# First mixture of a three-stage kernel: overflow blocks of all experts in one loop behind the last expert, rows written by indirect DMA

## Chip, core and metric

The kernel runs on one core of one Trainium2 chip. The metric is the device time of one execution in microseconds, the median of several runs. Engines are named as the profile names them: PE is TensorE (PEld its weight loads, PEq its sequencer), DVE is VectorE, ACT is ScalarE, POOL is GpSimd, SP is SyncE; SP issues most of the DMAs.

## What is computed

Attention, then a mixture of experts in which each token goes to one expert, then a second mixture in which each token goes to all eight. Cut to the part that the change touches:

```python
# attention: B=4, H=8, S=576, D=64, chunks of 64   -> x of (2304, 512)

def _moe_ref(x, w_gate, w1, w2, capacity):           # first mixture, capacity = 576
    logits = x @ w_gate
    expert_idx = np.argmax(logits, axis=1)           # one of E = 8 experts
    gate_w = ...                                     # its softmax probability
    for i in range(N):                               # tokens in order
        e = expert_idx[i]
        if counts[e] < capacity:                     # a full expert drops the token
            disp[e, counts[e]] = x[i]; pos[i] = counts[e]; counts[e] += 1; keep[i] = True
    h = np.maximum(np.einsum('ecd,edf->ecf', disp, w1), 0.0)    # D=512, F=1024
    y = np.einsum('ecf,efd->ecd', h, w2)
    out[i] = gate_w[i] * y[expert_idx[i], pos[i]]    # 0 for a dropped token

def _moe2_ref(x, w_gate, w1, w2):                    # second mixture
    P = exp(x @ w_gate - max), scaled 8 times to rows and columns of equal sums
    for e in range(E):
        out += P[:, e:e + 1] * (np.maximum(x @ w1[e], 0.0) @ w2[e])
```

With the inputs that are timed, the eight experts of the first mixture get 512, 128, 466, 384, 174, 128, 320 and 192 tokens. No expert has more than 512, and no token is dropped.

## The kernel before

The kernel is a single program. Attention runs until about 134 us of the span, the first mixture until 381 us, the second until the end. All products are made in 16-bit floats with a high and a low half of each operand (names `hi`, `lo`, `hh`, `hl`), so that one exact product is three matmuls.

**First mixture.** A loop in Python (`for x in range(E)`, unrolled in the program) runs over the experts. An expert's tokens are gathered from DRAM by index (`gather`, on POOL), turned by PE (`turn`, L338), and worked on in blocks of 128 rows by `blocks`. `blocks` makes the first product with `first_product` (L353 on PE; ACT and DVE make `hh` at L358 and `hl` at L359) and the second product (L896 on PE); then ACT squares the result (L900), DVE finds a power of two as scale (L89 to L92), ACT and DVE write the two halves of the row tile (L906, L907), and SP sends the row to `x2_d` (L909) and the row's scale and token number, `rkt`, to `rk_d` (L914). In the trace, the tile `x_d` is `x2_d`. The first product goes by four groups of the 1024 hidden columns.

Each expert has, in this order: a pair of blocks that always runs (tokens 0 to 255); `further(2)` inside an If with label `m` (more than 256 tokens, L1060; expert 0 has no such If); inside it `further(3)` in an If with label `n` (more than 384, L1063); and inside that `rest()` in an If with label `o` (more than 512, L1065). `rest` is a loop over the blocks from 512 on; for expert 0 it also recomputes the first two blocks if an earlier guess about which tokens are its own had found too few; for expert 7 it also starts two loads named `heads`. Tests are made on the engines' own registers, on every engine. An engine that skips a body runs a short list of semaphore updates in the body's place, and waits there for its own work before the If to be finished; the profile puts these under the If's line (L1060, L1063, L1065). With this run's counts, L1065's test is reached by experts 0 and 2 and skips in both; L1063 skips for experts 3 and 6, L1060 for experts 1, 4, 5 and 7.

**Work woven in.** `sites` is a list of lists of Python functions: between two groups of a block's first product, and behind each second product, `blocks` calls the functions of one list. They load, scale and split the next expert's weights: `w_scale` is a matmul against a matrix of ones that sums over partitions (`over_partitions`, L177), `w_scale2` is a chain of small DVE operations on it (L205, L89 to L92, L213), `w_split` writes a weight's two halves (ACT L254 or L246, DVE L255 or POOL). The order in which these calls are written is the order on each engine; every engine works through its queue in order.

**Second mixture.** It begins with transposes on PE of the first rows (L1171, on the tiles loaded by `heads`), casts of them on ACT and DVE into tiles `x` (L1181), and first products (L1283). Its tiles lie in pools that share memory with those of the first mixture.

## Time and profile before

| | |
|---|---|
| three runs | 1741.68, 1744.98, 1749.51 us |
| median | 1744.98 us |
| the profiled execution | 1743.53 us |
| its span | 1741.8 us |
| PE busy in the span | 97% |
| DVE, ACT, POOL busy | 69%, 55%, 42% |
| granted TensorE clock, mean | 0.997 |

The span is the profiled part of one execution; 1.7 us of that execution lie outside it. "Busy" counts matmuls, vector operations and the like, not branches, semaphore operations or DMA issues. Where an engine was idle before an operation, a timeline row gives the length in brackets, and behind the arrow what ended it; an engine's name with a q (PEq, DVEq) is that engine's sequencer, and the line behind it the line of the semaphore operation or branch. [...]

### The profile page before, as it was taken

How to read it: one execution, taken by the hardware profiler on the slowest of the kernel's cores; microseconds unless marked ns; L12 is line 12 of the kernel's file. 1: busy time of each engine (PE TensorE's matmuls, PEld its weight loads, DVE VectorE, ACT ScalarE, POOL GpSimd, SP SyncE). 2: the span in 40 equal slices, each digit the busy share in tenths (PEclk: the TensorE clock that was granted, in tenths of full speed). 3: DMA queues.
4: the chain of work that ended last, by engine and by line, in shares of the span. 5: the costliest groups of instructions: out<-in, count | busy, mean ns of one | idle time of the engine just before them, and what ended most of it. 6: DMA issues, size and time to landing. Idle time of an engine off the chain costs nothing.

```text
span 1741.8 us, 33426 instructions
## 1 busy us (share of the span) xinstructions
PE 1691.9 (97%) x13203; PEld 1224.7 (70%) x13203; DVE 1199.1 (69%) x2336; ACT 953.5 (55%) x1805; POOL 726.7 (42%) x765
## 2 busy tenths in 40 slices
PE   8889999989999999999999999999999999999997
PEld 6775666655555577777777777777777767777776
DVE  7886857755578666776676767677766686677554
ACT  6976756754445554665455545455644665354431
POOL 2335644622023243553445434453534543453443
PEclk9999999999999999999999999999999999999999
DMA  9948878745242413242233224323323241323201
GB/s 227 248 142 243 228 182 195 198 113 143 82 155 94 144 53 134 65 176 85 92 129 131 87 98 148 107 86 113 130 89 133 65 174 47 131 66 126 91 34 49
DMA packets 140344, 219.17 MB, mean 126 GB/s; under 512 B 62304, under 2 KB 80832, under 8 KB 140160
## 3 DMA queue, kind: packets, MB, share of 16 engines
q1 hardware_dynamic: 134768, 199.46, 36.6%
q0 software_dynamic: 5392, 17.26, 3.6%
q8 instruction: 115, 1.88, 0.5%
q14 instruction: 69, 0.57, 0.2%
HBM read 167.56 MB, written 41.91 MB: 120 GB/s over the span
## 4 chain that ended last, share of the span: by engine, by line
PE 69%; DVE 5%; ACT 2%; issue 1%; POOL 1%; POOLq 0%; ACTq 0%; DVEq 0%
PE p_m L1283 36%; PE p_m L1379 28%; PE p_m L1427 5%; DVE wall L297 3%; DVE acc L1350 1%; ACT wall L296 1%; PE p_m L1171 0%; ACT eh L1288 0%; POOL out_dram L1361 0%; DVE el L1291 0%; ACT tq L1323 0%; DVE tq L1298 0%; POOL el L1295 0%; DVE tq L1301 0%; DVE wall L255 0%
## 5 line engine op out<-in xcount | busy, mean ns | idle before, releaser
L1283 PE MATMUL p_m<-x,wall 128*128 128x384 f16 x4032 | 667.7, 326 | 4.9 <-ACT tq L1323 4.1
L1295 POOL TENSOR_TENSOR el<-tq,eh 128x384 f16<-128x384 f32 x336 | 346.8, 1060 | 568.6 <-ACT eh L1288 567.9
L1379 PE MATMUL p_m<-wall,eh 128*128 128x256 f16 x3528 | 580.3, 273 | 0.0
L1283 PEld LDWEIGHTS <-wall 128*128 128x128 f16 x4032 | 394.3, 98 | 262.6 <-issue 8.3
L1379 PE MATMUL p_m<-wall,el 128*128 128x256 f16 x1764 | 480.8, 273 | 0.0
L1288 ACT ACTIVATE eh<-tq 128x384 f16<-128x384 f32 x540 | 274.1, 522 | 190.2 <-DVE tq L1301 101.4
L1379 PEld LDWEIGHTS <-eh 128*128 128x128 f16 x3528 | 344.3, 98 | 44.4
L1350 DVE SCALAR_TENSOR_TENSOR acc<-p_m,cf,acc 128x256 f32<-128x256 f32 (+1 forms) x378 | 175.6, 521 | 130.7 <-PE p_m L1379 130.7
L1298 DVE TENSOR_TENSOR tq<-p_m,tq 128x384 f32<-128x384 f32 x288 | 158.4, 556 | 127.9 <-PE p_m L1283 126.8
L1379 PEld LDWEIGHTS <-el 128*128 128x128 f16 x1764 | 172.6, 98 | 19.9
L1291 DVE SCALAR_TENSOR_TENSOR el<-tq,eh 128x384 f16<-128x384 f32 x204 | 175.2, 860 | 10.0 <-ACT eh L1288 8.6
L1301 DVE SCALAR_TENSOR_TENSOR tq<-tq 128x384 f32<-128x384 f32 x252 | 133.1, 553 | 2.8
L353 PEld LDWEIGHTS <-wall 128*128 128x128 f16 x1344 | 107.3, 98 | 19.3 <-issue 7.2
L1323 ACT COPY tq<-p_m 128x384 f32<-128x384 f32 x96 | 45.6, 475 | 112.4 <-PE p_m L1283 109.9
L1427 PE MATMUL p_m<-wall,eh 128*128 128x512 f16 x288 | 85.6, 379 | 0.0
L275 POOL TENSOR_TENSOR tq<-stb 128x256 f32<-128x256 f32 x56 | 48.9, 873 | 81.9 <-DVE wsumsq L184 59.0
L1336 ACT ACTIVATE tq<-tq 128x384 f32<-128x384 f32 x84 | 43.9, 522 | 69.9 <-DVE tq L1298 69.9
L353 PE MATMUL p_p<-xT,wall 128*128 128x256 f16 x672 | 75.6, 272 | 3.7 <-DMA rk_d<-rkt 1.5
L296 ACT ACTIVATE wall<-stb,wsb 128x256 f16<-128x256 f32 (+1 forms) x56 | 31.3, 606 | 87.0 <-DMA wb_d<-wall 61.5
L275 POOL TENSOR_TENSOR tq<-sta 128x256 f32<-128x256 f32 x56 | 45.0, 804 | 72.8 <-DVE wall L297 43.3
L247 POOL TENSOR_SCALAR stb<-stb,wsb 128x1024 f32<-128x1024 f32 x16 | 53.6, 3350 | 52.0 <-DVE tq L1298 45.1
L297 DVE SCALAR_TENSOR_TENSOR wall<-stb,wsb,wall 128x256 f16<-128x256 f32 (+1 forms) x56 | 38.1, 690 | 50.9 <-ACT wall L296 48.1
(283 smaller groups left out, 2115.5 us busy)
## 6 DMA issues: line engine op xcount, KB each, us to landing
x<-xt_d SPq DMA_DIRECT2D x147, 384.0 KB
wb_d<-wall SPq DMA_DIRECT2D x20, 896.0 KB
wall<-wb_d SPq DMA_DIRECT2D x20, 896.0 KB
sta<-in_moe_w_dram SPq DMA_DIRECT2D x32, 512.0 KB
stb<-in_moe_w_dram SPq DMA_DIRECT2D x32, 512.0 KB
sta<-in_moe_w_dram SPq DMA_DIRECT2D x16, 1024.0 KB
stb<-in_moe_w_dram SPq DMA_DIRECT2D x16, 1024.0 KB
xt_d<-x SPq DMA_DIRECT2D x21, 384.0 KB
```

The costliest lines, as they stand in the source:

```text
L275: nc.gpsimd.tensor_tensor(out=at(o), in0=at(u), in1=at(v), op=op)
L297: nc.vector.scalar_tensor_tensor(out=o[:, cs, 1], in0=src, scalar=m.s, in1=o[:, cs, 0], op0=ALU.mult, op1=ALU.subtract)
L353: nc.tensor.matmul(p[:, f4, :], lhsT=w[:, kk, f * 128:(f + 1) * 128], rhs=xT[:, lo + kk, 0:W], start=(n == 0), stop=(n == 3 * KD - 1))
L1283: nc.tensor.matmul(p, lhsT=wt[:, w, lw, kk, :], rhs=xt[:, lx, kk, :], start=first and n == 0, stop=n == 5, skip_group_check=not first)
L1288: nc.scalar.activation(out=hs[op][0][:, q, :], in_=src, func=AF.Relu if op in (A11, A12, A22) or plain else AF.Copy)
L1291: nc.vector.scalar_tensor_tensor(out=hs[op][1][:, q, :], in0=src, scalar=0.0, in1=hs[op][0][:, q, :], op0=ALU.max, op1=ALU.subtract)
L1295: nc.gpsimd.tensor_tensor(out=hs[op][1][:, q, :], in0=src, in1=hs[op][0][:, q, :], op=ALU.subtract)
L1298: nc.vector.tensor_tensor(out=o, in0=a, in1=b, op=ALU.add)
L1301: nc.vector.scalar_tensor_tensor(out=o, in0=a, scalar=0.0, in1=b, op0=ALU.max, op1=op)
L1350: nc.vector.scalar_tensor_tensor(out=acc[:, j, cols], in0=y, scalar=coefs[x][:, j:j + 1], in1=acc[:, j, cols], op0=ALU.mult, op1=ALU.add)
L1379: nc.tensor.matmul(bk.t[:, cols], lhsT=hs[op][lh][:, q, t * 128:(t + 1) * 128], rhs=b.q[q][:, w, lw, :], start=m in (1, 5) and q == 0 and ...
L1427: nc.tensor.matmul(y.t, lhsT=h[:, kk % 4, c * 128:(c + 1) * 128], rhs=w[:, kk, :], start=(n == 0), stop=(n == 3 * KF - 1))
```

## The change

All eight Ifs with label `o` and their `rest()` are taken out, and the branch hints that belonged to them. One If with label `r` (more than 512 tokens in any expert, or expert 0 needs its recomputation) stands behind the last expert instead. Its body is a loop over the experts; for one with work left it loads both weight matrices again, scales and splits them, and loops over its blocks from `t0` on; each block's rows are written by indirect DMA from POOL at row numbers worked out on the chip. The weights go into new tiles of the pools `stage2` and `stage_b`. `heads(gpsimd)` stands at the end of this body, and the `heads` on SP at expert 7 tests the same number.

The loop needs a small table `left` (for each expert: tokens left, first block, count, first row, count again) and the number `e_any`. They are made for every run, by two functions put into the sites of expert 4: `redo_sum` into the first list and `tables` into the third. The two operations that made `e_count` and `e_more` before are gone. `blocks` gets an argument `put`, which takes the place of the two row DMAs in the loop alone.

```diff
         def counted():
-            nc.vector.tensor_copy(e_count, p_tab[:, 256:258])
             nc.vector.tensor_scalar(out=e_redo, in0=p_tab[:, 256:257], scalar1=255.0, scalar2=float(N),
...
-        nc.vector.tensor_tensor(out=e_more, in0=e_redo, in1=p_tab[:, 256:257], op=ALU.max)
...
+        redo = const.tile([128, 3], F32, name="redo")
+
+        def redo_sum():
+            nc.vector.tensor_tensor(out=redo[:, 0:1], in0=e_redo, in1=ident[:, 0:1], op=ALU.mult)
+            hold["redo"] = over_partitions(redo[:, 0:1], 300, 1)
+
+        def tables():
+            nc.vector.tensor_copy(redo[:, 0:1], hold.pop("redo"))
+            nc.vector.tensor_reduce(out=redo[:, 1:2], in_=reg_i[:, 0:E], axis=AX.X, op=ALU.max)
+            nc.vector.tensor_tensor(out=e_any, in0=redo[:, 0:1], in1=redo[:, 1:2], op=ALU.max)
+            nc.vector.tensor_copy(left[:, :, 0], reg_i[:, 0:E])
...
             def next_count():
                 if y < E:
                     counted_next.append(count(y))
+                if y == E - 1:
+                    more.append(count(0, e_any))
...
             if x == E - 1:
-                with tc.If(rc <= N - SB):
+                with tc.If(more[0] <= 512):
                     heads(nc.sync)
...
+            if x == 4:
+                sites[0].append(redo_sum)
+                sites[2].append(tables)
...
-                rc = count(0, e_more)
+                rc = count(0)
...
+                if y == E:
+                    sites[4].append(lambda: tc.mark_branch_hint_location("r", more[0] > 512, engines=[mybir.EngineType.PE]))
...
                 with tc.If(rc > 384, label=f"n{x}"):
-                    further(3, [[lambda: skip("o")], [], []])
-                    with tc.If(rc > 512, label=f"o{x}"):
-                        rest()
+                    further(3)
...
+        more = more[0]
+
+        with tc.If(more > 512, label="r"):
...
+            with tc.For_i(0, E, 1) as e:
+                cur = cp.tile([128, 5], I32, tag="cur", name="cur", bufs=1)
+                nc.vector.tensor_copy(cur, of[:, bass.ds(e * 5, 5)])
+                with tc.If(nc.values_load(cur[0:1, 0:1], min_val=0, max_val=N) > 512):
...
+                        m.st = pool.tile([128, m.kk, m.n], F32, tag="st" + nm, name=f"st{nm}r")
+                        m.mx = smw("wmx" + nm, [128, 4])
+                        nc.sync.dma_start(out=m.st, in_=w[bass.ds(e, 1), :, :].rearrange("o (k p) n -> p (o k) n", p=128))
...
+                        for d, src in ((x2_d, row), (rk_d, to)):
+                            nc.gpsimd.indirect_dma_start(out=d[:, :], out_offset=bass.IndirectOffsetOnAxis(ap=at_i, axis=0),
+                                                         in_=src, in_offset=None)
+
+                    with tc.For_i(t0, (c + 127) // 128, 1) as t:
...
+                        blocks("r", turn(gather([idx], "xgl", 1), "xTl", "c"), 1, None, y_bank="c", put=put)
+            heads(nc.gpsimd)
```

In the program the change shows at three places. The first is PE at the start of expert 4's block pair, between the first and the second group of the first product; `wmxa` and `wmxb` are the maxima of the next expert's weights, `ones` the matrix of ones. Before:

```order
L353 LDWEIGHTS wall
L353 MATMUL p_p<-xT,wall 128x256
L177 MATMUL p_sum<-wmxa,ones_85 128x4 [waits Activation_49]
L177 MATMUL p_sum<-wmxb,ones_85 128x4 [waits DVE_49]
L353 LDWEIGHTS wall
L353 MATMUL p_p<-xT,wall 128x256 [waits PE_49]
```

After:

```order
L353 LDWEIGHTS wall
L353 MATMUL p_p<-xT,wall 128x256
L177 MATMUL p_sum<-wmxa,ones_85 128x4 [waits Activation_49]
L177 MATMUL p_sum<-wmxb,ones_85 128x4 [waits DVE_49]
L177 MATMUL p_sum<-redo,ones_85 128x1 [waits DVE_49]
L353 LDWEIGHTS wall
L353 MATMUL p_p<-xT,wall 128x256 [waits PE_49]
```

A third small matmul stands in PE's queue, ahead of the second group, and it waits for DVE.

The second is DVE in the same stretch, where it works on the next expert's weights (`wall<-sta` is a piece of the low half of its first matrix) and makes `hl` of each group. Before:

```order
L213 TENSOR_TENSOR iw<-wia,wib 128x1 [waits DVE_49]
L255 SCALAR_TENSOR_TENSOR wall<-sta_4321,wsa,wall 128x1024 [waits Activation_49]
L359 SCALAR_TENSOR_TENSOR hl<-p_p,hh 128x512 [waits Activation_49]
L255 SCALAR_TENSOR_TENSOR wall<-sta_4321,wsa,wall 128x1024 [waits Activation_49] x2
L359 SCALAR_TENSOR_TENSOR hl<-p_p,hh 128x512 [waits Activation_49]
L255 SCALAR_TENSOR_TENSOR wall<-sta_4321,wsa,wall 128x1024 [waits Activation_49]
```

After:

```order
L213 TENSOR_TENSOR iw<-wia,wib 128x1 [waits DVE_49]
L255 SCALAR_TENSOR_TENSOR wall<-sta_3574,wsa,wall 128x1024 [waits DMAHW6_49,Activation_49]
L948 TENSOR_TENSOR redo<-e_redo,ident 128x1
L359 SCALAR_TENSOR_TENSOR hl<-p_p,hh 128x512 [waits Activation_49]
L255 SCALAR_TENSOR_TENSOR wall<-sta_3574,wsa,wall 128x1024 [waits DMAHW7_49,Activation_49]
L255 SCALAR_TENSOR_TENSOR wall<-sta_3574,wsa,wall 128x1024 [waits DMAHW2_49,Activation_49]
L359 SCALAR_TENSOR_TENSOR hl<-p_p,hh 128x512 [waits Activation_49]
L255 SCALAR_TENSOR_TENSOR wall<-sta_3574,wsa,wall 128x1024 [waits DMAHW3_49,Activation_49]
L952 COPY redo<-p_sum 128x1 [waits DVE_49]
L953 TENSOR_REDUCE redo<-reg_i 128x1
L954 TENSOR_TENSOR e_any<-redo 128x1 [waits DVE_49]
L955 COPY left<-reg_i 128x8
```

The operation that the new matmul waits for (L948) stands behind the first L255 and ahead of the second group's `hl`; the eleven operations of `tables` (L952 to L962, the first four of them shown) stand between the fourth L255 and the fourth group's `hl` (L359).

The third is ACT from the last expert into the second mixture, with the ends of the Ifs behind expert 7 (L1065, L1063, L1060 before; L1083, the If `r`, after) and the first casts of the second mixture (L1181 before, L1243 after). Before:

```order
L1055 UNCONDITIONAL_BRANCH x2
L1065 UNCONDITIONAL_BRANCH [waits Activation_49]
L1063 UNCONDITIONAL_BRANCH [waits Activation_49]
L1060 UNCONDITIONAL_BRANCH [waits Activation_49]
L1181 CAST x_8949<-p_m 128x384 [waits PE_49] x2
L1192 CAST x_8971<-p_m 128x384 [waits PE_49] x2
```

After:

```order
L1083 UNCONDITIONAL_BRANCH
L1083 UNCONDITIONAL_BRANCH [waits Activation_49,Activation_sequencer_49]
L1243 CAST x_7367<-p_m 128x384 [waits DVE_49,DMAHW7_49,PE_49,Activation_49]
L1243 CAST x_7367<-p_m 128x384 [waits PE_49]
L1254 CAST x_7389<-p_m 128x384 [waits PE_49] x2
```

The first cast waited for PE alone before, and now for DVE, for its own engine and for `DMAHW7`, the count of one of SP's DMA lanes; DVE's first cast has the same waits. In the skipped body of `r` this count comes from SP's list of updates (L1083), which stands behind SP's last row DMAs and behind its skip of expert 7's If `m` (L1060 before, L1073 after), and ahead of SP's load of `rk` (L1205 before, L1267 after).

## Rows read from the trace of the kernel before

**Rows 1.** Page: busy us, share of span, instructions; then the chain, by engine

```profile
PE 1691.9 (97%) x13203; PEld 1224.7 (70%) x13203; DVE 1199.1 (69%) x2336; ACT 953.5 (55%) x1805; POOL 726.7 (42%) x765
...
PE 69%; DVE 5%; ACT 2%; issue 1%; POOL 1%; POOLq 0%; ACTq 0%; DVEq 0%
```

**Rows 2.** Waits, 134 to 390 us: who, for whom, total us, times, longest

```profile
PE p_p L353 <- PEq L1065: 1.2, 2, 0.6
```

**Rows 3.** PE timeline where L1065 skips: start, us, operation, count, idle

```profile
171.87 0.50 PE L353 MATMUL p_p<-xT,wall 128*128 128x256 f16 x3 [0.60 <-PEq L1065]
...
242.00 0.60 PE L353 MATMUL p_p<-xT,wall 128*128 128x256 f16 x4 [0.56 <-PEq L1065]
```

**Rows 4.** PE timeline at the start of expert 4's block pair

```profile
275.35 2.78 PE L353 MATMUL p_p<-xT,wall 128*128 128x256 f16 x24 [0.56 <-DMA rk_d<-rkt]
277.96 0.28 PE L177 MATMUL p_sum<-wmxa,ones 128*128 128x4 f32 x2
278.11 0.36 PE L177 MATMUL p_sum<-wmxb,ones 128*128 128x4 f32 x2
278.33 0.71 PE L353 MATMUL p_p<-xT,wall 128*128 128x256 f16 x5
```

**Rows 5.** VectorE timeline of the same stretch

```profile
280.76 0.16 DVE L213 TENSOR_TENSOR iw<-wia,wib 128x1 f32<-128x1 f32 x1
281.19 1.29 DVE L255 SCALAR_TENSOR_TENSOR wall<-sta,wsa,wall 128x1024 f16<-128x1024 f32 x1 [0.27 <-ACT wall L254]
282.71 0.69 DVE L359 SCALAR_TENSOR_TENSOR hl<-p_p,hh 128x512 f16<-128x512 f32 x1 [0.23 <-ACT hh L358]
...
289.23 0.68 DVE L359 SCALAR_TENSOR_TENSOR hl<-p_p,hh 128x512 f16<-128x512 f32 x1
```

**Rows 6.** PE timeline, second products of expert 4

```profile
290.50 0.38 PE L896 MATMUL p_y<-wall,hl 128*128 128x512 f16 x1
```

**Rows 7.** Windows: PE, PEld, DVE, ACT, POOL busy, PEclk, DMA share, GB/s

```profile
130.00:132.00 2.00, 1.04 (x10) 0.85 (x10) 1.22 (x5) 0.00 (x0) 1.13 (x2) 1.00 0.96 341
...
385.00:386.00 1.00, 1.00 (x14) 0.83 (x12) 0.49 (x2) 0.60 (x2) 0.00 (x0) 0.67 0.39 129
386.00:387.00 1.00, 1.00 (x5) 0.50 (x4) 0.65 (x2) 0.35 (x1) 0.00 (x0) 0.50 0.25 17
387.00:388.00 1.00, 1.00 (x8) 0.66 (x7) 0.00 (x0) 0.09 (x1) 0.00 (x0) 0.50 0.00 0
388.00:389.00 1.00, 1.00 (x14) 1.00 (x13) 0.00 (x0) 0.39 (x1) 0.00 (x0) 0.62 0.00 0
```

**Rows 8.** PE timeline, a gap in the expert tables

```profile
130.34 0.22 PE L650 MATMUL p_tab<-cols,rows 128*128 128x144 f16 x1 [2.53 <-DVE wall L359]
```

**Rows 9.** PE timeline from the last expert into the second mixture

```profile
381.37 0.66 PE L1171 MATMUL p_m<-id,wall 128*128 128x128 f16 x9 [0.30 <-PEq L1060]
383.98 0.45 PE L1171 MATMUL p_m<-id,wall 128*128 128x128 f16 x5 [1.94 <-DVEq L1060]
...
385.63 0.85 PE L1283 MATMUL p_m<-x,wall 128*128 128x384 f16 x2
```

**Rows 10.** VectorE and ScalarE timelines there

```profile
384.01 1.02 DVE L1181 CAST x<-p_m 128x384 f16<-128x384 f32 x2
...
383.06 0.86 ACT L1181 CAST x<-p_m 128x384 f16<-128x384 f32 x2
```

**Rows 11.** SyncE timeline there (its DMA issues)

```profile
384.36 1.27 SPq L914 DMA_DIRECT2D rk_d<-rkt  x1
```

**Rows 12.** Line L1060, branches: count, ns min/median/max, first and last start

```profile
L1060 SPq EVENT_SEMAPHORE  x24: 17/17/17, 206.9 to 386.5; - x24
L1060 PEldq COMPARE_BRANCH  x7: 76/364/4182, 190.1 to 377.0; - x7
...
L1060 SPq COMPARE_BRANCH  x7: 34/45/53, 202.1 to 385.7; - x7
```

**Rows 13.** Line L1065, branches of the removed If on PE

```profile
L1065 PEldq COMPARE_BRANCH  x4: 196/534/3104, 167.6 to 241.6; - x4
```

More of the change, by code (lines that the diff above doesn't have):

```diff
@@ L328 @@
     e_kg = const.tile([128, 2], F32, name="e_kg")
-    e_count = const.tile([128, 2], I32, name="e_count")
-    e_more = const.tile([128, 1], I32, name="e_more")
+    e_any = const.tile([128, 1], I32, name="e_any")
+    left = const.tile([128, E, 5], I32, name="left")
     e_redo = const.tile([128, 1], F32, name="e_redo")
@@ L860, in turn, with blocks @@
             return xT, rows
-        def blocks(x, pre, nb, row0, sites=(), main=False, behind={}, y_bank="y"):
+        def blocks(x, pre, nb, row0, sites=(), main=False, behind={}, y_bank="y", put=None):
             b = mats[x, "b"]
@@ L908, in blocks @@
                                                op0=ALU.mult, op1=ALU.subtract)
-                nc.sync.dma_start(out=x2_d[bass.ds(row0(t), 128), :],
-                                in_=rhl.rearrange("p c l n -> p (c l n)").bitcast(F32))
-                to = tos[t]
+                to, row = tos[t], rhl.rearrange("p c l n -> p (c l n)").bitcast(F32)
+                if put is None:
+                    nc.sync.dma_start(out=x2_d[bass.ds(row0(t), 128), :], in_=row)
                 nc.vector.scalar_tensor_tensor(out=to[:, 0:1], in0=kg, scalar=inv, in1=iws[x],
                                                op0=ALU.mult, op1=ALU.mult)
-                nc.sync.dma_start(out=rk_d[bass.ds(row0(t), 128), :], in_=to)
+                if put is None:
+                    nc.sync.dma_start(out=rk_d[bass.ds(row0(t), 128), :], in_=to)
+                else:
+                    put(row, to)
                 site()
@@ L942 @@
         rows = gather(tokens(1, 0, 1))
+        redo = const.tile([128, 3], F32, name="redo")
[7 more added lines that the diff above has]
+            nc.vector.tensor_copy(left[:, :, 0], reg_i[:, 0:E])
+            nc.vector.tensor_scalar(out=left[:, 0, 0:1], in0=reg_i[:, 0:1], scalar1=redo[:, 0:1], scalar2=None, op0=ALU.max)
+            nc.vector.memset(left[:, :, 1], 4)
+            nc.vector.tensor_scalar(out=redo[:, 2:3], in0=redo[:, 0:1], scalar1=4.0, scalar2=-1.0, op0=ALU.min, op1=ALU.mult)
+            nc.vector.tensor_scalar(out=left[:, 0, 1:2], in0=redo[:, 2:3], scalar1=4.0, scalar2=None, op0=ALU.add)
+            nc.vector.tensor_scalar(out=left[:, :, 2], in0=reg_i[:, 0:E], scalar1=1.0, scalar2=None, op0=ALU.max)
+            nc.vector.tensor_copy(left[:, :, 3], reg_i[:, E:2 * E])
+            nc.vector.tensor_copy(left[:, :, 4], reg_i[:, 0:E])
+        hold, more = {}, []
         for x in range(E):
@@ L1041, in further @@
                 blocks(x, (late_t[:, :, (t - 2) * 128:(t - 1) * 128], late_r[t - 2:t - 1]), 1, lambda _: rank(t), sites)
-            def rest():
-                c = count(0) if x == 0 else rc
-                with tc.If(c > 512) if x == 0 else nullcontext():
-                    with tc.For_i(4, (c + 127) // 128, 1) as t:
-                        idx = cp.tile([128, 1], I32, tag="idx", name="idx")
-                        nc.vector.tensor_copy(idx, gidx[:, x, bass.ds(t, 1)])
-                        blocks(x, turn(gather([idx], "xgl", 1), "xTl", "c"), 1, lambda _: rank(t), y_bank="c")
-                if x == 0:
-                    with tc.If(nc.values_load(e_count[0:1, 0:1], min_val=0, max_val=N) <= 255):
-                        for t in range(2):
-                            blocks(x, turn(gather(tokens(0, t), "xgl", 1), "xTl", "c"), 1, lambda _, t=t: ranks(0)(t), y_bank="c")
-                if x == E - 1:
-                    with tc.If(c > N - SB):
-                        heads(nc.gpsimd)
             if x == 0:
```

34 lines of the change are left out of this document (33 added, 1 removed).

## The prediction, made before the changed kernel ran

> **What bounds the kernel now.** The page comes first: PE is busy for 97% of the span, and PE holds 69% of the chain that ended last [rows 1]. So an engine's added work costs time only where PE waits for it, and what is taken away is worth only the PE idle time that goes with it. The change touches the first mixture (134 to 381 us) and the step into the second. The waits of that stretch, read for PE, name the removed If: two waits behind L1065, 1.2 us in all [rows 2]. PE's timeline gives their places: 0.60 us ahead of the product at 171.87 (expert 0) and 0.56 us ahead of the one at 242.00 (expert 2) [rows 3]. The jumps themselves took PE's sequencer 0.2 to 3.1 us on this line [rows 13], so most of a jump lies under matmuls that are still queued, and only the wait for PE's own last work and the end of the jump show. The last view is the windows, for the granted clock: it is 1.00 nearly everywhere, and falls to 0.50 behind the gap of 1.94 us at the step into the second mixture [rows 7, 9].
>
> **What is removed.** Only experts 0 and 2 reach the old If `o` with these counts. Both gaps go: 0.60 + 0.56 = 1.16 us. The two skips that stay (`n` for experts 3 and 6, `m` for 1, 4, 5 and 7) have the same lists as before. Shorter code may shorten their jumps: at L1060, PE's run from 0.08 to 4.18 us [rows 12], but they were hidden except for an end such as the 0.30 us at 381.37 [rows 9], so I count nothing, with a bound of 0.5 us below. The two removed DVE operations are of one column, like the 0.16 us one in [rows 5], and lie where DVE has no PE work behind it; at most 0.15 us. Removed: 1.2 us, between 1.0 and 1.8.
>
> **The wait at expert 4.** The new matmul of `redo_sum` stands in PE's queue right behind the two L177 and waits for L948 on DVE, which stands behind the first L255. Before, PE made the second L177 at 278.11 and went on with the second group at 278.33, without a gap [rows 4]. DVE ran that L255 from 281.19 to 282.48 (1.29 us) [rows 5]. Behind it L948 takes about what the like operation at 280.76 took, 0.16 us [rows 5], so PE is released at 282.64. Its own tiny matmul costs about what the second L177 did until the next product, 278.33 - 278.11 = 0.22 us [rows 4]. The second group begins at 282.64 + 0.22 = 282.86 in place of 278.33: **+4.5 us**. Nothing on DVE's side can come sooner, since all that stands ahead of L948 there depends on the two L177 and on ACT, not on the group that PE holds back. Behind PE's queue head stand all later groups of this pair; ACT's `hh` and DVE's `hl` of the second group (282.71 before) wait with it. PE does not win this back, being the bound. The lower bound is 0, if the wait is hidden, for which I see no cover; the upper is 5.2, if the 0.27 us that L255 waited for ACT [rows 5] double and the weight load of the next group isn't done ahead.
>
> **The tables at expert 4.** Eleven operations stand on DVE ahead of the fourth group's `hl`. At 0.16 us each [rows 5] they take 1.8 us. That `hl` began at 289.23 and took 0.68, until 289.91, and PE first needed it at 290.50 [rows 5, 6]: 0.6 us of cover. ACT and DVE gain another 1 us or so while PE stands still, since they finish what they have queued for the next expert. So 0 to 1.2 us show; I take 0.3.
>
> **The clock behind the wait.** Behind the gap of 1.94 us that ended at 383.98, PE first ran at full clock; then the clock fell (385 to 386 has 0.67), stayed at 0.50 and came back in 388 to 389; the four windows lost 0.33 + 0.50 + 0.50 + 0.38 = 1.71 us of work [rows 7, 9]. Not every gap does this: behind 2.53 us of idle ahead of 130.34 the window 130 to 132 still has 1.00 [rows 7, 8]. A gap of 4.5 us is longer than both, and I take one such dip nearly in full, **+1.6 us**, between 0 and 3.4 (two in a row).
>
> **The step into the second mixture.** The first casts on ACT and DVE ran at 383.06 and 384.01 [rows 10], ended by 385.03, and PE went from its transposes to the first product at 385.63 without a wait [rows 9]. In the changed order these casts also wait for `DMAHW7`, which the skip of `r` on SP counts up. SP gets there late: it issues the last `rk_d` at 384.36 for 1.27 us, takes the branch of `m` at 385.7 and ends its list of six updates at 386.5 [rows 11, 12]. With `r`'s branch, jump and three more updates behind a list now shorter by two, at 0.35 to 0.9 us (0.87 being what the first skip took from 385.63 to 386.5), it ends at 386.9 to 387.4; I take 387.1. The casts take 1.02 us [rows 10], a tenth or two go to the semaphore, and the first product starts at 388.25 in place of 385.63: **+2.6 us**. PE's transposes are then done, so PE idles. If the first of the two casts is enough for the product to start, it is half a cast pair less, 2.1; if SP's jump goes slow, more (below). The other engines' own skips of `r` have room: DVE's first skip was over by 384.01 [rows 10], and a second as long as SP's 0.9 us ends by 384.9; PE's longest jump, 4.18 us [rows 12], set behind 381.37, would end at 385.6, and the transposes that then remain take 2 us, about until the casts are done. The clock dip that began in 385 to 386 [rows 7] now falls partly into the idle time, which gives back up to 1.3, and the second gap can bring another 1.7: I take 0.
>
> **Cover that costs nothing here.** The tables' number `e_any` is loaded at expert 6, long after expert 4. POOL and SP issue no more for `r` than a skip. PE's hint for `r` stands at expert 7, as the others did.
>
> **Sum.** -1.2 + 4.5 + 0.3 + 1.6 + 2.6 = **+7.8 us**. On the profiled execution, 1743.53 us with 1741.8 in the span, that is 1751.3; the median of the three runs lies 1.45 above that execution, and on it the forecast is 1744.98 + 7.8 = **1752.8 us**, 0.45% more. About 0.5% (8.7 us) is what a measurement of this kernel can tell from no change, so the likeliest outcome is "the same", just below that bound.
>
> **Rivals.** *Slower by more than the bound: SP's jump into the skip of `r` stalls.* This would decide at the casts, which nothing but SP releases. PE's longest jump on L1060 took 4.18 us [rows 12]; SP's own first skip took under 0.9. If SP's second jump takes 4.2 in place of about 0.5, the product starts 3.7 us later still: 7.8 + 3.7 = 11.5, 1756.5 us. It decides for "slower" from 0.9 us of extra jump on. For it: the body of `r` is the longest that SP has ever jumped over, and nothing hides SP. Against it: no jump of SP before was slow. [...]
> *Two dips in place of one* behind the 4.5 us wait or at the step: +1.7 on the sum, 1754.5, slower too.
> *The wait at expert 4 is not there*, because something releases L948 or the matmul sooner: then 4.5 and 1.6 fall away, +1.7, 1746.7 us, the same. For it: nothing but the small size of the operation. Against: DVE works its queue in order.
> *The step is covered* (the casts' wait ends with DVE's own skip, not SP's): 7.8 - 2.6 = +5.2, 1750.2, the same.
> *Faster:* the change acts as its removals alone, all new waits covered, and the shorter PE stream saves jumps elsewhere. The removals are worth 1.2 to 1.8 us, 1743.5; for more than 8.7 there is no row, so this can hardly go past "the same".
>
> **Chances.** The forecast case 0.62 (two thirds of it below the bound, since its terms spread by about 2 us around 7.8 and the runs before spread by 4); stalled jump or second dip 0.17; no wait at expert 4, or only removals, 0.10; step covered 0.08; a gain past the bound from something unseen 0.03. So slower 0.17 + 0.21 = 0.38, same 0.59, faster 0.03. The range leaves out 2 in 10: from 1748 (between 1746.7 and 1750.2) to 1758 (stalled jump, with a dip partly on top).
>
> **What would show it.** In the profile after: a gap of about 4.5 us on PE at expert 4, its releaser DVE, behind it windows at half clock; no PE wait behind the old If `o`; the first casts of the second mixture released by SP some 6 us past the end of the last `p_y` product; a PE gap of some 2.6 us ahead of the first product; the passes behind 400 us unchanged in length. The forecast is wrong if L948 runs ahead of L255, if SP's skip is slow, or if the second mixture itself runs at another speed.

## The result, and the profile after

| | before | after |
|---|---|---|
| first group: median (runs) | 1744.67 us (6) | 1758.24 us (6), 1752.5 to 1762.1 |
| ratio, 95% interval | | 1.0071, 1.0049 to 1.0093 |
| second group | 1746.81 us (35) | 1755.20 us (12), ratio 1.0043, 1.0022 to 1.0064 |
| third group | 1746.98 us (22) | 1754.97 us (11), ratio 1.0041, 1.0025 to 1.0057 |
| the profiled execution | 1743.53 us | 1757.8 us |
| its span | 1741.8 us | 1756.1 us |

The change makes the kernel slower. The first group says by 12.4 us (0.71% of 1744.67), the two larger groups by about 7.3 us (0.42%). All three intervals hold 0.5%, the bound between "the same" and "slower"; the forecast, 7.8 us, lies inside the intervals of the later two groups and below that of the first. The 1758.24 us of the first group are just past the upper end of the range, 1758.0.

The page after (span; busy us, share of the span, number of instructions):

```profile
span 1756.1 us, 33427 instructions
...
PE 1703.2 (97%) x13205; PEld 1234.1 (70%) x13205; DVE 1199.2 (68%) x2346; ACT 954.1 (54%) x1805; POOL 726.5 (41%) x765
```

PE has 11 us more of busy time than in [rows 1], with two more matmul records. That is clock and not work: of one product, PE made 11 matmuls from 288 to 290 us at a granted clock (PEclk, a share of full speed) of 0.50, called half clock below, and 21 from 292 to 294 at 1.00. Most of the 11 us doesn't come with the change: in a second profile of the changed kernel (a0, below) PE is busy for 1692.2 us, hardly more than before, and in the first 134.7 us of the one shown here the mean clock was 0.92, against 0.99 before.

The waits of 134 to 402 us, as in [rows 2] (engine, line, releaser, us in total, times, longest):

```profile
PE p_sum L177 <- DVE redo L948: 4.1, 1, 4.1
...
ACT x L1243 <- SPq L1083: 4.0, 1, 4.0
...
DVE x L1243 <- SPq L1083: 3.1, 1, 3.1
...
PE p_p L353 <- DMA rk_d<-rkt: 2.2, 2, 1.2
```

The If `o` has left the list, and the three waits that the change put in stand in it: PE for `redo`, and ACT and DVE for SP's skip of the If `r` (L1083).

**Expert 4.** PE's timeline after, the counterpart of [rows 4]:

```profile
281.57 0.36 PE L177 MATMUL p_sum<-wmxb,ones 128*128 128x4 f32 x2
286.07 0.58 PE L177 MATMUL p_sum<-redo,ones 128*128 128x1 f32 x2 [4.13 <-DVE redo L948]
286.51 1.23 PE L353 MATMUL p_p<-xT,wall 128*128 128x256 f16 x5
```

The second L177 starts at 281.57 and the next product at 286.51: 4.94 us, where it was 0.22. That is 4.7 us more, against 4.5 in the forecast, with the releaser that was named. What the clock did behind it, in windows (busy us of PE, PEld, DVE, ACT, POOL, then PEclk, DMA share, GB/s):

```profile
284.00:286.00 2.00, 0.00 (x0) 0.00 (x0) 1.70 (x5) 1.66 (x2) 0.24 (x1) 0.55 0.99 127
286.00:288.00 2.00, 1.93 (x10) 1.50 (x11) 0.01 (x1) 0.00 (x0) 2.00 (x1) 0.50 0.41 83
288.00:290.00 2.00, 2.00 (x11) 1.44 (x10) 0.00 (x0) 0.00 (x0) 1.92 (x2) 0.50 0.83 304
290.00:292.00 2.00, 2.00 (x16) 1.58 (x15) 0.00 (x0) 0.49 (x1) 0.87 (x1) 0.75 1.31 278
```

PE comes back at 286.07 to a clock of 0.50, and has it until 291.0. By those 11 matmuls in 2 us against 21, about half of that time, 2.5 us, is lost.

DVE in the same stretch, the counterpart of [rows 5], and POOL and PE beside it:

```profile
285.86 0.15 DVE L948 TENSOR_TENSOR redo<-e_redo,ident 128x1 f32<-128x1 f32 x1
...
298.04 0.15 DVE L952 COPY redo<-p_sum 128x1 f32<-128x1 f32 x1
...
298.29 0.16 DVE L954 TENSOR_TENSOR e_any<-redo 128x1 int32<-128x1 f32 x1
298.37 0.37 DVE L955 COPY left<-reg_i 128x8 int32<-128x8 int32 x1
...
299.10 0.15 DVE L959 TENSOR_SCALAR left<-redo 128x1 int32<-128x1 f32 x1
299.17 1.78 DVE L960 TENSOR_SCALAR left<-reg_i 128x8 int32<-128x8 int32 x1
...
300.94 0.16 DVE L962 COPY left<-reg_i 128x8 int32<-128x8 int32 x1
301.01 0.68 DVE L359 SCALAR_TENSOR_TENSOR hl<-p_p,hh 128x512 f16<-128x512 f32 x1
```

```profile
285.76 2.90 POOL L247 TENSOR_SCALAR stb<-stb,wsb 128x1024 f32<-128x1024 f32 x1 [2.09 <-ACT w L246]
...
295.87 2.85 POOL L247 TENSOR_SCALAR stb<-stb,wsb 128x1024 f32<-128x1024 f32 x1 [5.00 <-ACT w L246]
298.80 2.13 POOL L248 TENSOR_TENSOR w<-stb,w 128x1024 f16<-128x1024 f32 x1
```

```profile
301.75 0.39 PE L894 MATMUL p_y<-wall,hl 128*128 128x512 f16 x1 [0.72 <-DVE hl L359]
```

L948 ends at 286.01, right before PE goes on. Of the tables' eleven operations, nine take between 0.07 and 0.21 us, near the 0.16 that was costed. The other two work on eight columns and end with an operation of POOL's: L955 takes 0.37 and ends at 298.74, POOL's L247 at 298.72; L960 takes 1.78, from 299.17 until 300.95, and POOL's L248 ends at 300.93. Behind that, L962, a copy of the same size, takes 0.16. From L952 to the fourth `hl` it is 2.97 us (298.04 to 301.01). The fourth `hl` comes late by that much, and PE waits 0.72 us for it ahead of 301.75.

**The step into the second mixture**, the counterparts of [rows 9], [rows 10] and [rows 12]:

```profile
394.40 0.66 PE L1233 MATMUL p_m<-id,wall 128*128 128x128 f16 x9 [1.08 <-DVE x2h L89]
396.23 0.45 PE L1233 MATMUL p_m<-id,wall 128*128 128x128 f16 x5 [1.16 <-DVEq L1073]
...
399.73 1.76 PE L1345 MATMUL p_m<-x,wall 128*128 128x384 f16 x5 [0.96 <-ACT x L1243]
```

```profile
399.20 0.86 ACT L1243 CAST x<-p_m 128x384 f16<-128x384 f32 x2 [4.00 <-SPq L1083]
```

```profile
L1083 SPq EVENT_SEMAPHORE  x3: 17/17/17, 398.9 to 399.1; - x3
...
L1083 SPq COMPARE_BRANCH  x1: 45/45/45, 398.5 to 398.5; - x1
```

SP takes the branch of `r` at 398.5, and its last update is at 399.1; ACT's first cast starts at 399.20, after 4.00 us of waiting, and the first product at 399.73. The last `p_y` product ended at 393.32, so this took 6.41 us, against 385.63 - 381.07 = 4.56 before. The half clock, in windows:

```profile
396.00:397.00 1.00, 0.77 (x13) 0.78 (x14) 0.11 (x1) 0.00 (x0) 0.00 (x0) 0.92 0.12 47
397.00:398.00 1.00, 1.00 (x12) 1.00 (x11) 0.00 (x0) 0.00 (x0) 0.00 (x0) 0.50 0.58 201
...
402.00:403.00 1.00, 1.00 (x13) 1.00 (x11) 0.00 (x0) 0.45 (x1) 0.00 (x0) 0.50 0.45 6
403.00:404.00 1.00, 1.00 (x15) 1.00 (x14) 0.00 (x0) 0.23 (x1) 0.00 (x0) 0.67 0.91 33
```

It begins late in 396 to 397 and ends in 403 to 404: two spells of the length of the one in [rows 7], of which 0.96 us fall into the gap ahead of 399.73.

**By stages.** The profiles of all kernels, cut at four places that each of them has: the first `p_y` product (the end of attention and tables), the first `p_y` of expert 3, the first `p_y` of expert 4, and the last `p_y`. In us; the last column is what the change can touch.

| kernel | until first p_y | experts 0 to 2 | to expert 4's p_y | to the last p_y | to the end | from first p_y to the end |
|---|---|---|---|---|---|---|
| before | 134.8 | 118.1 | 33.3 | 94.9 | 1360.8 | 1607.1 |
| before, again (b0) | 139.3 | 116.6 | 33.7 | 95.5 | 1361.0 | 1606.8 |
| after | 141.8 | 113.9 | 40.9 | 96.8 | 1362.8 | 1614.3 |
| after, again (a0) | 136.5 | 116.2 | 40.7 | 96.5 | 1363.0 | 1616.4 |
| after, again (a1) | 136.9 | 114.1 | 40.4 | 96.8 | 1362.9 | 1614.1 |
| b1, no If `o` | 136.2 | 120.1 | 33.4 | 96.0 | 1360.9 | 1610.3 |
| b2, before with tables | 136.7 | 116.9 | 39.4 | 97.1 | 1359.4 | 1612.9 |
| e1, L948 early | 136.6 | 119.3 | 38.7 | 97.2 | 1362.8 | 1618.1 |
| e2, loads on POOL | 140.4 | 114.1 | 40.7 | 97.2 | 1360.6 | 1612.5 |
| e3, e1 and e2 | 137.9 | 114.1 | 37.2 | 98.2 | 1359.1 | 1608.6 |
| e4 | 136.8 | 114.8 | 35.2 | 96.3 | 1359.5 | 1605.8 |
| e5 | 141.9 | 115.3 | 33.6 | 94.4 | 1359.5 | 1602.7 |
| e5, again | 137.8 | 114.1 | 34.4 | 96.1 | 1360.4 | 1605.0 |
| e6, e5 with a hint | 135.1 | 112.7 | 33.6 | 96.2 | 1360.5 | 1602.9 |

Until the first `p_y` no instruction changed but the removed DVE operations, and that part alone runs from 134.8 to 141.9 us. In the profile after, ACT waited there for a weight load (row of ACT's timeline):

```profile
42.02 1.06 ACT L168 ACTIVATE wsq<-sta 128x1024 bf16<-128x1024 f32 x1 [3.06 <-DMA sta<-in_moe_w_dram]
```

PE had no work for 2.83 us behind it, until 43.96, and from 46 to 52 us the granted clock was 0.50. The spread stands between profiles of one and the same kernel: 134.8 and 139.3 us in before, 136.5 to 141.8 in after, 137.8 and 141.9 in e5. It is several us wide, so two groups of six runs may well lie 12 us apart where the larger ones lie 7, and the last column tells more than one total. That column has a spread too, 2.3 us in the three profiles of after and 2.3 in the two of e5.

### The profile page after: what moved, and what is told of

Read it like the earlier page. It is cut to its first block, busy times and chain, and to the rows that moved or that the text cites. A ratio compares the mean times of both kernels' runs of the same rounds, so it can differ in the third digit from the quotient of the medians.

```text
span 1756.1 us, 33427 instructions
## 1 busy us (share of the span) xinstructions
PE 1703.2 (97%) x13205; PEld 1234.1 (70%) x13205; DVE 1199.2 (68%) x2346; ACT 954.1 (54%) x1805; POOL 726.5 (41%) x765
## 4 chain that ended last, share of the span: by engine, by line
PE 68%; DVE 5%; ACT 2%; issue 1%; POOL 1%; POOLq 0%; ACTq 0%; DVEq 0%
PE p_m L1345 35%; PE p_m L1441 27%; PE p_m L1489 5%; DVE wall L297 3%; DVE acc L1412 1%; ACT wall L296 1%; PE p_m L1233 0%; ACT eh L1350 0%; POOL out_dram L1423 0%; DVE el L1353 0%; ACT tq L1385 0%; POOL el L1357 0%; DVE tq L1360 0%; DVE tq L1363 0%; DVE wall L255 0%
## 5 line engine op out<-in xcount | busy, mean ns | idle before, releaser
L247 POOL TENSOR_SCALAR stb<-stb,wsb 128x1024 f32<-128x1024 f32 x16 | 52.7, 3295 | 60.4 <-DVE tq L1360 48.4
```

## The experiments

**The kernel before, again (b0).** No edit.

> The kernel before, unaltered, for a second profile of it. Theory (the changed kernels are later by 2 to 7 us when the first p_y starts only because the profile of before caught a quick attention): its first p_y starts at 136 to 142 us as in the five profiles of changed kernels (141.8, 136.5, 136.6, 140.4, 137.9), not at 134.8, and from there to the end it takes 1607 us again within 1.5. Rival (attention is slower in the changed kernel by the placement of its tiles): it starts at 134 to 135.5 again.

The first `p_y` came at 139.3 us, and from there to the end it took 1606.8 us against 1607.1. So nothing here shows attention to be slower in the changed kernel; the first profile of before had the quickest of all fourteen. Its median was 1747.88 against 1746.40 of the others of its group, ratio 0.9993 (0.9973 to 1.0013).

**The changed kernel, again (a0 and a1).** No edit.

> The changed kernel once more, unaltered, as the base of this group. Theory: its median is 12 to 14 us above the kernel before; of the 14.3 us in its profiled span about 5.4 lay in attention and the token tables (no instruction changed there), 7 to 8 at expert 4, 2 to 3 at the step into the second mixture. If attention's share is chance, this profile will show another share there, and the same two gaps (about 4.1 us at expert 4, about 1 us ahead of the first product of the second mixture).

> The changed kernel a third time, in the group with e5. Theory: 7 to 9 us above the kernel before and above e5 by 8 to 10; from the first p_y to the end 1614 to 1617 us again; the time of the first p_y anywhere from 134 to 142. In its tables, the operation L960 (TENSOR_SCALAR on eight columns) again takes far over 0.2 us wherever POOL's L248 runs beside it. Rival (the 8 us belong to the drawing of runs): within 4 us of before.

1755.20 and 1754.97 us, 8.4 and 8.0 above the medians of before. In both profiles the 4.13 us gap at the matmul on `redo` and 0.71 at the `hl` behind it stand again, and L960 took 1.78 us in both. The three profiles of after average 1614.9 us in the last column, before 1606.9: **+8.0 us**, with attention left out. The gap at the step was 0.96, 2.37 and 1.24 us in the three; PE's transposes ahead of it ended 5.45 us behind the last `p_y` in after (6.41 - 0.96) and 4.58 in a0 (6.95 - 2.37).

**The kernel before without the If `o` (b1).** Its body (blocks from 512 on, expert 0's recomputation, heads of that body) is left out.

```diff
-                    further(3, [[lambda: skip("o")], [], []])
-                    with tc.If(rc > 512, label=f"o{x}"):
-                        rest()
+                    further(3)
```

> The kernel before without the If o and its body (the blocks from 512 on, expert 0's recomputation and the heads of that body are left out); nothing is put in their place. Theory: the two PE gaps at L1065 (0.60 and 0.56 us) go and nothing else changes: 1 to 1.5 us less than before, not to be told apart by the times alone but to be seen in the profile. Rival (what the Ifs cost is far more, by code that is skipped): over 4 us less.

The median was 1744.76 us, ratio 0.9993 (0.9972 to 1.0014): no gain that can be told. Both gaps at L1065 are gone, but experts 0 to 2 took 120.1 us, 3 more than before. PE's timeline and two windows of that stretch, expert 0's third block:

```profile
164.55 0.39 PE L353 MATMUL p_p<-xTc,wall 128*128 128x128 f16 x4 [0.49 <-issue]
165.31 0.44 PE L353 MATMUL p_p<-xTc,wall 128*128 128x128 f16 x5 [0.37 <-issue]
...
168.26 1.55 PE L353 MATMUL p_p<-xTc,wall 128*128 128x128 f16 x13 [0.77 <-issue]
...
166.00:168.00 2.00, 1.25 (x10) 0.88 (x10) 0.00 (x0) 0.00 (x0) 1.05 (x2) 0.56 1.06 124
168.00:170.00 2.00, 1.74 (x17) 1.73 (x17) 0.69 (x1) 0.60 (x1) 0.00 (x0) 0.50 0.93 329
```

PE got its matmuls there in batches of four or five, with gaps called issue (waiting for nothing that the profile shows), and then had half clock. e1 has the same (119.3 us), and e5 four gaps of 0.32 to 1.02 us; after, a0, a1, e2, e3 and e4 have two to four of 0.18 to 0.55, b2 one of 0.47; before, b0, e5 again and e6 have none there. So what the skip of expert 0 cost was often paid again as gaps of this kind. In the kernel after, experts 0 to 2 took 2.6 us less than before on average (114.7 against 117.4), more than the 1.2 of the two gaps: there, waits of PE on DVE and ACT at experts 1 and 2 (0.80, 0.50 and 1.09 us in before) got shorter, too: the first two are gone in all three profiles of after, and the third is 0.30. They don't go with the moved If alone, since b1 still has 0.55 and 1.12 of them, and b2, which keeps the Ifs, 0.62 and 0.30. Why they move isn't known.

**The kernel before with the tables (b2).** `redo_sum` and `tables` at expert 4 as in the change, the Ifs `o` kept, nothing uses the table.

```diff
+            if x == 4:
+                sites[0].append(redo_sum)
+                sites[2].append(tables)
```

> The kernel before with redo_sum and tables added at expert 4 at the places of the change; the Ifs o stay, nothing uses the table. Theory: the PE gap of 4.1 us in front of the matmul on redo stands here too, with windows at half clock behind it and a gap of 0.7 to 1 us at the fourth hl: 6 to 8 us more than before. Rival (the time comes with the moved If, not with the tables): under 3 us more.

1754.07 us against 1746.40, ratio 1.0032 (1.0013 to 1.0050). The wait is there alone:

```profile
283.38 0.59 PE L177 MATMUL p_sum<-redo,ones 128*128 128x1 f32 x2 [4.14 <-DVE redo L949]
```

The column to expert 4's `p_y` has 39.4 us, 5.9 more than the 33.5 of before, with one spell of half clock of 3.4 us in place of the 6.8 in after, a0 and a1 (40.4 to 40.9). Behind the last `p_y` it loses nothing against before (1359.4). So what `redo_sum` and `tables` do at expert 4, not the moved If, is what costs most.

**L948 moved ahead (e1).**

```diff
-        def redo_sum():
+        def redo_first():
             nc.vector.tensor_tensor(out=redo[:, 0:1], in0=e_redo, in1=ident[:, 0:1], op=ALU.mult)
+
+        def redo_sum():
             hold["redo"] = over_partitions(redo[:, 0:1], 300, 1)
...
+            if x == 3:
+                sites[1].append(redo_first)
```

> The DVE operation of redo_sum (L948) is moved from expert 4's first site list to expert 3's second; the matmul and the tables stay. Theory (the wait and the half clock behind it are 4.5 + 2.5 to 3.3 us): the 4.1 us PE gap at expert 4 goes, no half clock there, and the time falls by 7 to 8 us, to about 1750 to 1751. Rival (the extra time is mostly from the first 135 us, by another placement of tiles): the gap goes but the time falls by 4 to 5 us at most and stays above 1753.

This missed: 1755.67 us, no gain, ratio to before 1.0043 (1.0026 to 1.0061). A second wait stood behind the first. PE's timeline, and L948's own row (count, ns min/median/max, first and last start):

```profile
284.89 0.38 PE L177 MATMUL p_sum<-redo,ones 128*128 128x1 f32 x2 [1.69 <-DVE wmmb L205]
```

```profile
L948 DVE TENSOR_TENSOR redo<-e_redo,ident x1: 2095/2095/2095, 255.9 to 255.9; 128x1 f32<-128x1 f32 x1
```

The matmul on `redo` writes into the tile `p_sum` that the two L177 have just written and that DVE reads at L205; it now waits 1.69 us for that read. So 1.69 of the 4.13 us were never L948's alone. And L948 itself, 0.15 us in after, takes 2.10 us at expert 3 and pushes DVE's work there back. The column to expert 4's `p_y` came down only from 40.7 to 38.7, and e1's gaps at expert 0 took that back in its profile. What the 2.10 us go with is seen in e4 and e5.

**The weight loads of `r` on POOL (e2).** The casts' wait for a count of SP's becomes one for a count of POOL's.

```diff
-                        nc.sync.dma_start(out=m.st, in_=w[bass.ds(e, 1), :, :].rearrange("o (k p) n -> p (o k) n", p=128))
+                        nc.gpsimd.dma_start(out=m.st, in_=w[bass.ds(e, 1), :, :].rearrange("o (k p) n -> p (o k) n", p=128))
```

> The two weight loads in the body of the If r are issued by POOL in place of SP, so that the first casts of the second mixture wait for POOL's skip (some 20 us earlier) in place of SP's. Theory: the casts are released by DVE's skip, 2 us earlier; the gap of about 1 us ahead of the first product goes, and with the shorter half clock the time falls by 1 to 3 us, to about 1756. Rival (the casts are bound by something else at the same time, as the transposes at half clock are): no change within 0.7 us.

PE's first product and ACT's first cast in e2; then the first product in a0, from the same group:

```profile
397.65 1.17 PE L1345 MATMUL p_m<-x,wall 128*128 128x384 f16 x3
...
396.03 0.86 ACT L1243 CAST x<-p_m 128x384 f16<-128x384 f32 x2 [1.78 <-DVEq L1083]
```

```profile
396.89 1.51 PE L1345 MATMUL p_m<-x,wall 128*128 128x384 f16 x6 [2.37 <-ACT x L1243]
```

The cast is released by DVE's skip now, after 1.78 us of waiting in place of 4.00, and PE goes from its transposes to the product without a gap, 5.28 us behind the last `p_y` (6.95 in a0). To the end it takes 1360.6 us, as in before. The median, 1753.48, is 1.7 below a0's, in the expected range, though less than the runs' spread. The casts' wait for SP is the cost of the step, 2.0 to 2.3 us.

**Both (e3).** The edits of e1 and e2.

> Both edits of the last two together: no wait at expert 4, casts not released by SP. Theory: what is left is the removals (-1.2) and the tables (up to +1): 1744 to 1746, no more than 1 us from the kernel before. Rival (attention is slower in the changed kernel for good): 1749 to 1750, 5 us above the kernel before, and the extra time stands ahead of 136 us.

1753.47 us, ratio 1.0033 (1.0014 to 1.0052): above what was expected. The profiled execution, 1748.06 us, is one of the quick ones of its twelve, 5.4 under their median, so it can account for a part of the loss only. It says 1608.6 us from the first `p_y`, 1.6 us over before: 3.7 of it stand ahead of expert 4's `p_y` (37.2 against 33.5; L948's 2.09 us and the 1.69 us wait) and 3.0 behind it (98.2 against 95.2; a gap of 2.25 us at the `hl` behind the tables), against gains in experts 0 to 2. The rival, a slower attention, isn't what this profile shows (first `p_y` at 137.9 us).

**The matmul ahead, the small table (e4).** On top of e3:

```diff
-                sites[0].append(redo_sum)
+                sites[0].insert(0, redo_sum)
...
+        def table():
             nc.vector.tensor_copy(left[:, :, 0], reg_i[:, 0:E])
...
         with tc.If(more > 512, label="r"):
+            table()
```

> As e3_both, and two edits more: the matmul on redo stands ahead of the two sums of the weights in place of behind them, where it waited for the DVE reads of p_sum (1.69 us left in e1 and e3), and eight of the eleven operations of tables (all but those that make e_any) are moved into the body of the If r. Theory: no PE wait at expert 4 at all, no gap at the fourth hl beyond what before had, no half clock there, no wait for SP at the step: 0.5 to 1.5 us less than before from the first p_y on, 1745 to 1748 as median against some 1747 of before. Rival (something else in the changed program costs 3 to 5 us): it stays 3 us or more above before, with the time in neither of the two places.

1748.22 us, ratio 0.9999 (0.9981 to 1.0018): the loss is gone. In the profile (its execution, 1744.23, is the quickest of the twelve) there is no gap at the matmul on `redo`, and 1605.8 us in the last column. Yet the column to expert 4's `p_y` has 35.2, 1.7 above before. DVE's timeline, and POOL's:

```profile
251.60 2.09 DVE L948 TENSOR_TENSOR redo<-e_redo,ident 128x1 f32<-128x1 f32 x1
...
289.91 0.82 DVE L956 TENSOR_TENSOR e_any<-redo 128x1 int32<-128x1 f32 x1
```

```profile
251.01 2.67 POOL L248 TENSOR_TENSOR wall<-stb,wall 128x1024 f16<-128x1024 f32 x1
...
285.71 2.94 POOL L248 TENSOR_TENSOR w<-stb,w 128x1024 f16<-128x1024 f32 x1
288.65 3.81 POOL L247 TENSOR_SCALAR stb<-stb,wsb 128x1024 f32<-128x1024 f32 x1
```

L948, one column wide, ends at 253.69; POOL's L248, which began ahead of it, ends at 253.68. The operation that makes `e_any` ran from 289.91 to 290.73, beside POOL's L247 (288.65 to 292.46) and ending with nothing of POOL's, so the expectation's "each ending with L248" holds for the first alone. What held the second isn't known: in after, the same operation beside the same line of POOL's (L954 at 298.29, L247 until 298.72) took 0.16.

**One tile and a scalar in place of two tiles (e5).** On top of e4:

```diff
-            nc.vector.tensor_tensor(out=redo[:, 0:1], in0=e_redo, in1=ident[:, 0:1], op=ALU.mult)
+            nc.vector.tensor_scalar(out=redo[:, 0:1], in0=ident[:, 0:1], scalar1=e_redo, scalar2=None, op0=ALU.mult)
...
-            nc.vector.tensor_tensor(out=e_any, in0=redo[:, 0:1], in1=redo[:, 1:2], op=ALU.max)
+            nc.vector.tensor_scalar(out=e_any, in0=redo[:, 1:2], scalar1=redo[:, 0:1], scalar2=None, op0=ALU.max)
```

> As e4_early_small, with L948 and the operation that makes e_any written with one operand as a per-partition scalar (TENSOR_SCALAR on one tile) in place of TENSOR_TENSOR on two. In e4 these two took 2.09 and 0.82 us, each ending with POOL's TENSOR_TENSOR L248, where such an operation alone takes 0.15. Theory (an operation of DVE with two tiles from memory waits until POOL's two-tile operation is over): both take 0.14 to 0.16 us at the same places, the 1 us that expert 3 lost in e1, e3 and e4 goes, and from the first p_y to the end it is 1604 to 1605 us against 1605.8 in e4 and 1607 in the two profiles of before. Rival (any operation at those places waits, whatever its form): 2.09 and 0.82 again, and 1605.8 again. The median can't tell these apart: 1745 to 1748.

> e5_scalar_form once more, for the comparison with e6 and for its own distance to the kernel before. Theory: 1 to 4 us less than before; from the first p_y to the end 1602 to 1606 us; short waits called issue in expert 0's last first product again. Rival (the 1.8 us of its first group were chance): within 1 us of before or above.

The two operations, at the same places in the program:

```profile
L948 DVE TENSOR_SCALAR redo<-ident,e_redo x1: 205/205/205, 257.1 to 257.1; 128x1 f32<-128x1 f32 x1
...
L956 DVE TENSOR_SCALAR e_any<-redo x1: 215/215/215, 293.8 to 293.8; 128x1 int32<-128x1 f32 x1
```

L948 began at 257.1 this time, and POOL's L248 ran from 256.51 to 259.18 beside it:

```profile
256.51 2.67 POOL L248 TENSOR_TENSOR wall<-stb,wall 128x1024 f16<-128x1024 f32 x1
```

They took 0.21 us each in place of 2.09 and 0.82, and the column to expert 4's `p_y` is 33.6 and 34.4, that of before. So at these two places it was the form of the operation, one tile and a scalar in place of two tiles, with the same operation of POOL's beside it. POOL's operation matters as well: in after, a0, a1, b2 and e2, L948 in its first form began about 0.1 us behind POOL's L247 (285.76 in after) and took 0.15 us. It was long only beside L248, which itself reads two tiles. The medians were 1745.22 us, ratio 0.9984 (0.9965 to 1.0002), and 1743.29 us, ratio 0.9981 (0.9967 to 0.9996): 2 to 3 us less than before, which the first interval can't tell from nothing, and 9.8 less than the changed kernel in the same group (a1). This version keeps all that the change does without its loss, and may beat the kernel before by a little.

**A hint (e6).** On top of e5, PE's branch hint for expert 1's If `m` stands in expert 0's third block.

```diff
-                    further(3)
+                    further(3, [[lambda: tc.mark_branch_hint_location("m1", counted_next[0] > 256, engines=[mybir.EngineType.PE])], [], []] if x == 0 else ())
...
-                sites[3].append(lambda: skip("m"))
+                if x > 1:
+                    sites[3].append(lambda: skip("m"))
```

> As e5_scalar_form, with PE's branch hint for expert 1's If m moved forward from expert 1 into expert 0's third block (further(3)), where the kernel before had the hint for its If o. Theory (PE has short waits for its own instruction stream there since that hint is gone, and they eat what the missing skip of expert 0 gave): the waits called issue in expert 0's last first product go, and from the third block's p_y start of expert 0 to the first p_y of expert 1's pair it takes 27 to 28 us as in before (27.9), against 28.4 to 33.5 in the eight profiles without the If o. Rival (it is the length of the code, or the DMA traffic alone): 28.4 us or more, with the same short waits. In the median 0 to 2 us less than e5.

Expert 0's third block to expert 1's pair took 27.1 us without gaps called issue, as expected of the hint. But e5 again, without it, took 27.1 us too, and had none. So this doesn't tell whether the hint does it; the gaps come and go between runs of one kernel. The medians were 1744.10 (ratio 0.9989, 0.9974 to 1.0003) and 1743.29. What makes these gaps stays open.

## Why the prediction came out as it did

The forecast was +7.8 us, with "the same" a little likelier than "slower". The profiles without attention say +8.0, the two larger groups of runs about +7.3 (ratios of 1.0043 and 1.0041), the first group +12.4. The sum was right; its terms, from the stage table (means of three profiles of after and two of before), were each off by 0.6 to 1.4 us:

| term | forecast | measured |
|---|---|---|
| the removed skips | -1.2 | -2.6 in experts 0 to 2 |
| PE's wait for L948 and the half clock behind it | +4.5 + 1.6 | +7.1 to expert 4's p_y |
| tables | +0.3 | +1.5 from there to the last p_y |
| the step | +2.6 + 0 | +2.0 behind the last p_y |
| sum | +7.8 | +8.0 |

The errors, -1.4, +1.0, +1.2 and -0.6, nearly cancel. They have different causes, so that the sum came out within 0.2 us is luck; that the wait at expert 4 and the step would make up the loss was not.

*The removed skips.* The two gaps of [rows 3] went, as forecast. The stage gained more in after and lost 2.7 in b1, so the term was right for what it named, and blind to what stands around it: short waits on DVE that shrink, and gaps at expert 0 that come.

*The wait at expert 4.* The place, the releaser and the size held: 4.7 us against 4.5. What the working missed is a second cause hidden under the first: it took the 0.22 us behind the second L177 as the price of a matmul that writes `p_sum`, but this one comes after the reads of L205, and would have waited about 1.7 us for them even with L948 out of the way (e1). It changed nothing in the sum; with L948's 2.10 us at its new place, it made the first repair fail.

*The clock.* One dip, 1.6 us, was costed from [rows 7]. Half clock followed this wait in all five profiles that have it, for 6.8 us in after, a0, a1 and e2 (2.5 us lost behind PE's return in after), and for 3.4 us in b2. So the term was short by about 1 us; the bound of 3.4 held it. Why one profile has half of the spell isn't known.

*The tables.* The mis-sized term: 1.8 us were put down for eleven operations of 0.16 us, and the cover of 0.6 us plus a gain of 1 was to hide most. From the first of them to the fourth `hl` it was 2.97 us. Ten of them together kept under their price; L960 alone took 1.78 us and ended with POOL's L248. PE's gap was 0.72 us, inside the bound of 1.2, and only this much is shown to be the tables'. The stage lost 1.5; the rest of it stands in short waits at experts 5 and 6, such as 0.97 us for ACT's `hh` at 363.02, where before had 0.17 at 350.36, and e4, which runs eight of the eleven operations elsewhere, has that wait too. The price of 0.16 us came from one row of another operation, of one column ([rows 5]), at a place where POOL ran neither L247 nor L248, and the text did not ask what POOL does at the new place.

*The step.* Right in mechanism: the casts were released by SP's skip of `r`, 5.9 us behind the last `p_y` product (399.2 - 393.32) where about 6 was forecast. The product needed only ACT's first cast, which is the 2.1 us bound that was given, so the time behind the last `p_y` grew by 1.85 us up to the first product. SP's jump into the skip took from 398.5 to the first of its updates at 398.9, so the rival of a stalled jump fell: SP's whole skip, from 398.5 to 399.1, took 0.6 us where 0.35 to 0.9 were put down.

*The chances.* The rival "two dips in place of one" (1754.5 us) came nearest to the 1755.0 and 1755.2 of the larger groups, and its mechanism is there: at expert 4 and at the step, the profile after has a spell of twice the length of the one in [rows 7]. But the nearness in time is chance, since the base was low by 2 us: in the larger groups before has medians of 1746.4 to 1747.0 in place of 1744.98, and from there the forecast's own +7.8 comes to 1754.2 to 1754.8. What the range lacked is the spread of attention, the first `p_y` being anywhere from 134.8 to 141.9 us; the single profile of before that the forecast went by had the earliest of all. By that spread a group of six runs can lie some us off, and the first group's 1758.24 came out a little above the range.

## What to carry to other kernels

A tiny operation cost here what stood ahead of it in its engine's queue (L948 took 0.15 us, and PE waited 4.13 for it): before putting a cross-engine pair (a DVE operation, then a matmul on it) into the bound engine's stream, place the producer a stage earlier, and the consumer ahead of others on the same tile, since the tile's readers were a wait too (1.69 us in e1, none in e4). The skipped branch of `r` still cost 2.0 to 2.3 us here, where its body's tiles give memory to what follows: choose the queue that loads them by when that queue's own skip is done (ACT's first cast waited 4.00 us with SP, 1.78 with POOL in e2). And when small operations are added on DVE, look at what POOL runs at that moment; where two tiles aren't needed, one tile and a scalar was the quicker form here (0.21 us in place of 2.09), though an operation on eight columns of one tile (L960) was long as well.

## What the runs showed of the hardware

- A DVE operation of one column that reads two tiles (L948) took 2.09 us beside POOL's L248, an operation on two tiles, and ended within 0.02 us of it (e1, e3, e4); written with one tile and a scalar, it took 0.21 at the same place (e5, e5 again, e6). Beside POOL's L247, on one tile and a scalar, the two-tile form took 0.15 (after, a0, a1, b2, e2).
- DVE operations on eight columns of one tile ended with POOL's operations too. The copy L955 took 0.37 us in after, a0, a1, b2 and e2 and 0.44 in e1 and e3 (under other line numbers in b2, e1 and e3), and ended 0.02 to 0.04 us behind L247 each time; alone, the like copy L962 took 0.16. L960 took 1.78 us, ending 0.02 to 0.04 behind L248, in all seven profiles that run it there; no run had it away from POOL, so that POOL held it is read from the ends and not tested. Neighbours on one column beside the same L248 (L959) took 0.15.
- The operation that makes `e_any`, on two columns of `redo`, took 0.16 us beside L247 in after (L954) and 0.82 beside L247 in e4 (L956); with one of the two as a scalar it took 0.21 beside L247 in e5. What makes L954 short, and L955 and L960 long, isn't shown.
- Half clock behind the same 4.1 us wait of PE lasted 6.8 us in four profiles (after, a0, a1, e2) and 3.4 us in one (b2).
- Between the profiles here, the attention part moves by up to 7 us (134.8 to 141.9 until the first `p_y`), and by 4 to 5 between profiles of one kernel (before, after, e5).
